# Centering two pairs of rows on the way to TensorE and applying their scale behind the matmul, in a LayerNorm, linear-attention and FFN kernel

## The chip, the cores and the metric

The kernel runs on one core of one Trainium2 chip. Five engines work side by side, each through its own queue in order: TensorE (PE, matrix products; PEld is its loading of weights), VectorE (DVE), ScalarE (ACT, functions such as Exp and Mish), GpSimd (POOL) and SyncE (SP, which here only issues DMA transfers). They wait for each other through semaphores. PE writes to PSUM, which has 8 banks of 512 float32 columns; ACT and DVE read it from there. The metric is the device time in microseconds, the median of several runs.

## The reference

One input x of 2048 rows and 448 columns (bf16) is normalized and goes through two branches that are added to it:

```python
xn = layernorm(x)                      # (x - mean) / sqrt(var + 1e-5), row by row
# A: linear attention, 16 heads of 28
q, k, v = split(xn @ wqkv)             # per head
pq, pk = q @ w_phi[h], k @ w_phi[h]
phi_q = concat(softmax(pq), softmax(-pq))
phi_k = concat(softmax(pk), softmax(-pk))
kv, z = phi_k.T @ v, sum(phi_k)
A = (phi_q @ kv) / (phi_q @ z + 1e-6) @ wo
# B: FFN with Mish
h = xn @ w1 + b1                       # 448 -> 1792
B = (h * tanh(softplus(h))) @ w2       # 1792 -> 448
out = x + A + B
```

## The kernel before

The rows lie as 16 tiles t of 128 rows; two tiles are a pair u (0 to 7). A function for each step of the work gives instructions to the engines, and the text `ORDER` (L147) names the steps one after the other: each engine's queue is the order in which the steps name it. Waits are worked out from what each instruction reads and writes (`Program.resolve`). So a step's place in `ORDER` is a place in several queues at once, and says nothing of time.

The steps, by their names in `ORDER`:

- `lx2s` and the like issue loads on SP: `lx`n rows of x from pair n on (x4 and x6 hold two pairs each), `lkm` and `lvm` rows 0 to 383 of the key and value weights, `lkt` the last 64 rows of both (loaded twice, for the upper and the lower half of the partitions, L276), `lp` the small per-head matrices, `lqT` the query weights transposed by DMA, `l1m`, `l1t`, `l2`, `lo` the FFN's and the output's weights. `lba` loads the bias.
- `z12` (`warm`, L359): twelve matmuls on a tile of zeros at the start.
- `st`u (`ln_stats`, L449): mean and variance of a pair, by bn_stats and bn_aggr on DVE; `st2b` and `st3b` do the odd tile on ACT (a Copy and a Square, each summing along the row). `rs`u (`ln_rstd`, L467): 1/sqrt(var + eps), on ACT (`a`) or POOL (`p`).
- `xn`u (`ln_pair`, L481): the normalized pair, on DVE (`d`) or POOL (`p`), in three pieces. It goes to one of four buffers xn.
- `xt`u (`xT`, L514): turns the pair into xnT, features on partitions: by PE, emptied by ACT and DVE (`b`) or by ACT (`a`), or by a DMA transpose on SP (`m`). Pairs 2 and 3 are turned by PE, six by DMA.
- `wtk`h, `wmk`h, `wmq`h (L545, L568): fold the per-head matrices into the key and query weights: Wk is turned by PE (8 transposes each for h = 0, 1), then multiplied (8 matmuls), the result emptied to Wpk or Wpq.
- `v`, `k`, `q` with a pair's number and a part (L609, L615, L677): the products of a pair with value, key and query weights; each is 28 matmuls of 64 rows by 448 columns, two of them at a time on the two halves of PE, given out in parts A (12), H (4), B (12) that may stand apart in `ORDER`. The last part's step empties the pair of banks: values by a copy (`a` on ACT, `d` on DVE), keys by two Exp on ACT (of plus and minus), written to E, and queries likewise to Eq.
- `kn`u.s (`k_norm`, L623): the key softmax's sums and reciprocals on DVE, the product on POOL. `kv`u adds the pair's part of kv; `kvz` copies it, and a DMA transpose turns it into KVZ.
- `e`t turns a tile of query exponentials by DMA; `nd`t forms numerator and denominator (16 matmuls, then DVE); `ot`u turns the result by DMA; `wo`u multiplies with wo.
- `f`q.n with parts A, H, B: the FFN's first product for half q of the rows and 128 of the 1792 features; `mish` on ACT empties it to actT. `g`t: the second product. `sto`u, `stt`t: stores.

PSUM banks are taken in pairs, the least recently used free pair first (`take2`, L380); a part holds its pair until its last step. A pair may be written again once the engines that read it have done so. Rows 6 to 13 of actT hold E until the FFN's features overwrite them, rows 4 and 5 hold Eq.

All matmuls of `v`, `k`, `q` and `f` have one line in the profile, L423 (they differ by their operands), the transposes of Wk L556, the products with the per-head matrices L580, those of xn L505.

Of the kernel before, what the change touches and what calls it, by code (L numbers as in the profile page):

```python
# [978 lines left out]
```

## Time and profile before

| what | value |
|---|---|
| median of 3 runs | 151.34 us (151.34 to 151.38) |
| span of the profiled execution, first to last instruction | 148.7 us |
| median less span | 2.6 us |
| HBM read, written | 7.02 MB, 1.84 MB |
| DVE, POOL busy in the span | 102.4 us, 38.8 us |
| the 16 DMA engines, queue q1 | 53.4% of their span |

The profile is of one execution. "Busy" counts instructions from start to end, so PE's share says that it always has a matmul in flight and not that it works at its peak. A line of a group reads: line, engine, operation, result<-operands, shapes, count, then busy time and the mean of one. In the timeline a row reads: start, time to the end of the last, engine, line, operation, count, and in brackets the idle time before it with what ended it. In the chain of waits a row reads: start, length, engine and line; from the last instruction back it follows what released each step.

### The profile page before, as it was taken

The page shows a single profiled execution, that of the slowest core. Times are in us where ns is not written, and L with a number is a line of the kernel's source. Part 1 is how long each engine was busy: PE and PEld are TensorE (multiplying, and loading weights), DVE is VectorE, ACT ScalarE, POOL GpSimd, SP SyncE. Part 2 cuts the span into 40 slices and gives each one's busy share as a digit, 9 for nine tenths or more (in the row PEclk, how much of TensorE's full clock was granted, in tenths as well). Part 3 has the DMA queues.
Part 4 walks back from the last instruction along what each step waited for, and adds up shares of the span by engine and source line. Part 5 has one row for each costly group of instructions (what it writes and reads, how often), then busy time and mean ns, then how long its engine had stood idle before and what let it go on. Part 6 is the DMA issues. An engine that isn't in the chain of part 4 may idle for free.

```text
span 148.7 us, 3867 instructions
## 1 busy us (share of the span) xinstructions
PE 144.3 (97%) x1669; PEld 74.4 (50%) x1669; DVE 102.4 (69%) x229; ACT 74.5 (50%) x91; POOL 38.8 (26%) x53
## 2 busy tenths in 40 slices
PE   6999999999999999999999999999999999999993
PEld 2375555555544554444544445545555555555562
DVE  0599898996999940407697879539983999930072
ACT  3987999879999999657757762002000000000000
POOL 4423475079999993000000000000000000000000
PEclk9999999999999999999999999999999999999999
DMA  4998678799499159399856053120013040542005
GB/s 133 240 270 232 138 143 158 128 169 334 102 194 191 30 49 132 69 223 283 225 120 121 0 66 62 27 39 0 7 21 102 20 108 0 123 100 85 4 0 185
DMA packets 39964, 17.23 MB, mean 116 GB/s; under 512 B 33932, under 2 KB 39180, under 8 KB 39948
## 3 DMA queue, kind: packets, MB, share of 16 engines
q1 hardware_dynamic: 39776, 16.89, 53.4%
q8 instruction: 13, 0.21, 0.6%
q10 hardware_dynamic: 172, 0.10, 0.2%
q14 instruction: 3, 0.02, 0.0%
HBM read 7.02 MB, written 1.84 MB: 60 GB/s over the span
## 4 chain that ended last, share of the span: by engine, by line
PE 96%; DVE 1%; POOL 0%; issue 0%; POOLq 0%
PE PS L423 50%; PE PS L828 29%; PE PS L845 7%; PE PS L364 4%; PE PS L722 3%; PE PS L649 2%; PE PS L580 1%; DVE xn L497 1%; PE PS L505 1%; DVE x_all L793 0%; POOL v_all L339 0%; PE PS L556 0%; DVE x_all L814 0%; DVE b1T L512 0%; PE PS L693 0%
## 5 line engine op out<-in xcount | busy, mean ns | idle before, releaser
L423 PE MATMUL PS<-xnT,W 64*128 64x512 bf16 x392 | 44.8, 377 | 0.0
L828 PE MATMUL PS<-W,actT 128*128 128x448 bf16 (+1 forms) x224 | 42.9, 351 | 0.0
L699 ACT ACTIVATE actT<-PS,b1T 128x1024 bf16<-128x1024 f32 x28 | 29.8, 1112 | 22.1 <-PE PS L423 22.1
L828 PEld LDWEIGHTS PS<-W,actT 128*128 128x128 bf16 x224 | 21.5, 98 | 19.8 <-issue 0.3
L423 PEld LDWEIGHTS PS<-xnT,W 64*128 64x128 bf16 x392 | 18.0, 94 | 21.9 <-PE PS L423 1.9
L630 POOL TENSOR_TENSOR actT<-actT,rSk 128x896 bf16<-128x896 bf16 x16 | 26.6, 1699 | 5.1 <-DVE rSk L628 5.1
L793 DVE TENSOR_TENSOR x_all<-PS,x_all 128x448 bf16<-128x448 f32 (+1 forms) x16 | 9.2, 614 | 15.1 <-PE PS L845 10.5
L626 DVE TENSOR_REDUCE Sk<-actT 128x32 f32<-128x896 bf16 x16 | 16.6, 1037 | 1.1 <-ACT actT L618 1.1
L618 ACT ACTIVATE actT<-PS 128x896 bf16<-128x896 f32 x16 | 13.7, 920 | 1.8 <-PE PS L423 1.7
L423 PE MATMUL PS<-Wpk,xnT 64*128 64x448 bf16 x112 | 13.2, 349 | 0.0
L423 PE MATMUL PS<-Wkv,xnT 64*128 64x448 bf16 x112 | 12.9, 349 | 0.0
L423 PE MATMUL PS<-Wpq,xnT 64*128 64x448 bf16 x112 | 12.6, 349 | 0.0
L738 DVE COPY Sq<-PS 128x16 f32<-128x16 f32 x32 | 4.0, 167 | 12.0 <-PE PS L722 12.0
L462 DVE BATCH_NORM_STATS2 stats<-x_all 128x6 f32<-128x448 bf16 x14 | 8.4, 601 | 3.5 <-DMA x_all<-in_A_x_dram 3.5
L746 DVE TENSOR_TENSOR v_all<-v_all 128x464 f32<-128x464 f32 x16 | 10.3, 642 | 0.6
L742 DVE TENSOR_TENSOR v_all<-PS,Sq 128x464 f32<-128x464 f32 x16 | 10.3, 641 | 0.5
L749 DVE TENSOR_TENSOR xn<-v_all,rden 128x448 bf16<-128x448 f32 x16 | 10.0, 626 | 0.6
L744 DVE TENSOR_TENSOR v_all<-PS,Sq 128x464 f32<-128x464 f32 x16 | 10.1, 630 | 0.0
L680 ACT ACTIVATE actT<-PS 128x896 bf16<-128x896 f32 x10 | 8.6, 930 | 0.1
L423 PEld LDWEIGHTS PS<-Wpq,xnT 64*128 64x128 bf16 x112 | 5.4, 94 | 5.0 <-ACT actT L680 0.2
L423 PEld LDWEIGHTS PS<-Wkv,xnT 64*128 64x128 bf16 x112 | 5.4, 94 | 5.0 <-ACT actT L618 0.2
L423 PEld LDWEIGHTS PS<-Wpk,xnT 64*128 64x128 bf16 x112 | 5.4, 94 | 5.1 <-issue 0.2
(83 smaller groups left out, 119.3 us busy)
## 6 DMA issues: line engine op xcount, KB each, us to landing
W<-in_B_w_dram SPq DMA_DIRECT2D x1, 1568.0 KB, 9.3
out_dram<-x_all SPq DMA_DIRECT2D x7, 224.0 KB, 2.2
W<-in_B_w_dram SPq DMA_DIRECT2D x1, 1344.0 KB, 6.5
x_all<-in_A_x_dram SPq DMA_DIRECT2D x4, 224.0 KB, 3.0
x_all<-in_A_x_dram SPq DMA_DIRECT2D x2, 448.0 KB, 4.7
Wkv<-in_A_wqkv_dram SPq DMA_DIRECT2D x2, 336.0 KB, 5.1
Wo<-in_A_wo_dram SPq DMA_DIRECT2D x2, 336.0 KB, 5.9
W<-in_B_w_dram SPq DMA_DIRECT2D x2, 224.0 KB, 3.6
```

Source lines behind the costliest of these rows:

```text
L423: ins = e.matmul(o, lhs(c, k), rhs(c, k), start=first and n == at[par][0], stop=last and n == at[par][-1])
L618: op("ACT", lambda e, s=s: e.activation(E_of(u)[:, s, :, :], two(b, D), ACT.Exp, scale=1.0 if s == 0 else -1.0), r=[pb(b), pb(b + 1)], w=[ ...
L626: op("DVE", lambda e: e.tensor_reduce(Sk[u][:, s, :], Eh(), AX.X, ALU.add), r=[("E", u, s)], w=[("Sk", u, s)], tag=f"Sk{u}.{s}")
L630: op("POOL", lambda e: e.tensor_tensor(Eh(), Eh(), ap_on(rSk[u][:, s, 0:1], [[1, 2 * H], [0, DH]]), ALU.mult), r=[("E", u, s), ("rSk", u, ...
L699: op("ACT", lambda e: e.activation(actT[:, fc, q * 1024:(q + 1) * 1024], bank(b, 2), ACT.Mish, bias=b1T[:, fc:fc + 1]), r=[("b1T",), pb(b) ...
L742: op("DVE", lambda e: e.tensor_tensor(tv(t1[i]), num(0), sx(1), ALU.mult), r=[pb(b), pb(b + 1), ("Sq", i, 1)], w=[("t1", i)], tag=f"ta{t}")
L744: op("DVE", lambda e: e.tensor_tensor(tv(t2), num(1), sx(0), ALU.mult), r=[pb(b), pb(b + 1), ("Sq", i, 0)], w=[("t2",)], tag=f"tb{t}")
L746: op("DVE", lambda e: e.tensor_tensor(t1[i], t1[i], t2, ALU.add), r=[("t1", i), ("t2",)], w=[("t1", i)], tag=f"tc{t}")
L749: op("DVE", lambda e: e.tensor_tensor(o_sb[(t // 2) % 2][:, t % 2, :].rearrange("p (h d) -> p h d", d=DH), t1[i][:, :, 0:DH], ap_on(rden[i ...
L793: op("DVE", lambda e: e.tensor_tensor(x_all[:, t, 0:n], bank(b)[:, 0:n], x_all[:, t, 0:n], ALU.add), r=[pb(b), ("x", t)], w=[("out", t)], ...
L828: ins = e.matmul(bank(b)[:, 0:width(t)], actT[:, fc, tok(t)], W2[:, fc, 0:width(t)], start=first and fc == 0, stop=last and fc == FC - 1)
L845: ins = e.matmul(bank(b)[:, 0:w], oT_of(u)[lo:hi, cc * P:(cc + 1) * P], Wo[lo:hi, cc, 0:w], start=first and n == at[par][0], stop=last and ...
```

## The change

In words:

- For pairs 2 and 3 (`CENT`) the rows are only centered (`xc`t, `center`), by DVE: x minus the mean for the even tile, x plus ACT's negative mean for the odd one. `st_mean` writes that negative mean to `nmean`. PE turns the centered pair (`ct`u, `xcT`) into row 3 of actT, emptied by ACT and DVE. Values and keys of these pairs are computed from it, and rstd is applied when they leave PSUM: values by one scaled copy for each tile, keys by four Exp with scale rstd or -rstd (`nrstd`), where there were two.
- For their queries and the FFN, pairs 2 and 3 are also normalized as before (`xn3p`, `xn2d`) and turned by DMA (`xt3m`, `xt2m`): all eight pairs now take that way.
- Statistics are given tile by tile (`sd`, `sm`, `sv` in place of `st`). The key and value weights' last 64 rows: the lower half of the partitions gets only the value part; Wk's last transposes read 64 rows, and the copy writes the result twice.
- The warm matmuls, six in place of twelve, read a constant of ones that exists from the start.
- `wmk0` and both `wmq` are emptied by ACT (before by ACT and DVE, and `wmq0` by DVE). The first empties of values are shared out anew: ACT has v3, v2, v1, v7, v5, v0 and DVE v6, v4 (before ACT v2, v3, v0, v6, v7). rstd of pairs 2, 1, 0 is on ACT, the rest on POOL; POOL normalizes pairs 3, 6, 5, DVE 1, 4, 7, 2, 0.
- A new `ORDER`. All query exponentials stand ahead of the first Mish.

The diff, cut to its core:

```diff
-pv table lx2s lba zero pm st2b lx3s lkms lps st3b lkts z12 pi b1 rs2p pw rs3a xn2d bd lx1s wtk0b lvms lx4s xn3d xt2b
-wtk1b wmk0b lqT2 xt3a v2Ha wmk1a v2Ba lqT0 st1 v3Ha lqT1 lqT3 rs1a v3Aa v2Aa st4 rs4p pk v3Ba k3H lx0s k3A qd xn1d
-wmq0d wmq1a k2H k3B lx6s pp k2A st5 q3A xn4d k2B q3B rs5p q2A xt1m l1ts q3H k1A q2H xn5p xt4m st0 v1Ad k1H st6 xt5m e7
...
+pi lx2s lba sd4 lx3s table pk z6 sm5 sv5 pw lkms xc4d b1 lps lt0s sm7 xc5d lt1s sd6 lvms pm rs2a xc7d lx1s bd lqT2
+sv7 xc6d rs3p ct2 lx6s lqT3 wtk0b lx4s wtk1b ct3 sd3 wmk0a xn3p wmk1a sd2 nr2d rs1a sd13 v3Ha xn1d sd12 v2Aa sd11 pp
+v2Ha lqT0 lqT1 v2Ba k2A rs6p k2H k3H k2B qd nr3d xn6p v3Aa k3A v3Ba wmq1a wmq0a xt1m xt3m sd10 sd8 k3B k1A lx0s v1Ha
+v1Bd xt6m sd9 k1H v1Aa sd14 q3H l1ts q3A sd15 rs4p q3B rs7p xn4d sd0 xn7d rs5p k1B xn5p sd1 xt4m q1H v6Bd v6Ad xn2d
+xt7m q1A q1B k6H k6B kn2.0 e6 v6Hd k4H kn3.1 xt2m k6A kn2.1 k4A pv k7A k4B v7Bd v7Hd rs0a kn4.0 e3 k7H q4H xn0d v7Aa
...
+k0H e9 q2B k0A q7H kn4.1 k0B v0Ad v0Ba q0H kn3.0 q0B q0A f1.3H e4 q7B q7A q5A kn1.1 q5H f1.3A e5 kn5.1 f1.2H e1 ep
+e0 kn6.1 q5B f1.3B f1.2B f0.2A f0.2H f0.0B f0.2B f0.0A f1.2A e15 kn5.0 f0.0H kn0.1 f1.13A l2s kn7.0 kn1.0 f0.1B
+f1.13H kv2 kn7.1 kv3 kv4 kn0.0 kv6 e10 kv7 kv1 kv5 kv0 f1.13B f0.12H kvz f0.1A f0.12A f0.1H f0.12B f1.8B f1.8H f1.1H
...
+sto6 sto2 sto4 stt14 g15 stt15
```

```diff
+    def load_kv_tail(eng, i):
+        (lo, hi), at = HALF[i], (0, D)[i]
+        dma(eng, lambda e: e.dma_start(Wkv[lo:hi, 3, at:2 * D], A_wqkv[384:448, D + at:3 * D]), w=[("Wt", i)],
+            tag=("ldWkv", "ldWvt")[i])
...
-                ins = e.matmul(bank(b)[:, :], ap_on(zeros[:, 0:1], [[0, P]]), ap_on(zeros[:, 0:1], [[0, TCW]]), start=True,
-                               stop=True)
+                ins = e.matmul(bank(b)[:, :], ap_on(ones, [[0, P]]), ap_on(ones, [[0, TCW]]), start=True, stop=True)
...
+    def st_mean(t):
+        i = t // 2 % 2
+        op("ACT", lambda e: e.activation(junk[i][:], x_all[:, t, :], ACT.Copy, scale=-1.0 / D, accum_out=nmean[:, t:t + 1]),
+           r=[("x", t), ("junk", i)], w=[("nm", t), ("junk", i)], tag=f"sm{t}")
...
+    def center(t, eng):
+        u = t // 2
+        for n, (lo, hi, at) in enumerate(parts_of_row(t)):
...
+            op(eng, lambda e, lo=lo, hi=hi, at=at: e.tensor_scalar(
+                xn[u % NXN][:, at:at + hi - lo], x_all[:, t, lo:hi], mean_of(t), None, op0=mean_op(t)),
+               r=[("x", t), mean_res(t)], w=[("xn", u % NXN, t % 2, n)], tag=f"xc{t}.{n}")
...
+    def xcT(u):
+        i = u % NXN
+        b = take2(False)
+        pe(lambda e: transpose7(e, b, xn[i], 3), [("xn", i, 0, 0), ("xn", i, 1, 0), ("xn", i, 1, 1), ("ident",)],
+           [pb(b), pb(b + 1)], f"xT{u}c")
+        for eng, lo, hi, bb, n in (("ACT", 0, 3, b, 0), ("DVE", 3, 7, b + 1, 1)):
+            at = (u % 2) * 7 * P
+            evac(eng, lambda lo=lo, hi=hi: actT[:, CROW, at + lo * P:at + hi * P],
...
+                    n = 64 if 2 * h + c == 3 else P
+                    ins = e.transpose(oT(c, n)[:, g, :], Wk[0:n, 2 * h + c, g * GP:(g + 1) * GP], ident[0:n, 0:n])
...
+    def scaled(eng, dst, src, t, r, w, tag):
+        if eng == "ACT":
+            op("ACT", lambda e: e.activation(dst(), src(), ACT.Copy, scale=rstd[:, t:t + 1]), r=r, w=w, tag=tag)
...
     def k_mm(u, part):
         def then(b):
+            if u in CENT:
+                for s in range(2):
+                    for i in range(2):
+                        op("ACT", lambda e, s=s, i=i: e.activation(
+                            E_of(u)[:, s, i, :], bank(b + i)[:, 0:D], ACT.Exp,
+                            scale=(rstd, nrstd)[s][:, 2 * u + i:2 * u + i + 1]),
+                           r=[pb(b + i), ("rstd", u), ("nrstd", u)], w=[("E", u, s)] if i else [("Eh", u, s)],
+                           tag=f"exkc{u}.{s}{i}")
+                return
```

More of the change, by code (lines that the diff above doesn't have):

```diff
@@ L227, in _kernel, with xcT_of @@
     FE = FC - NU
+    CENT = (2, 3)
+    CROW = 3
+    def xcT_of(u, c):
+        return actT[:, CROW, (u % 2) * 7 * P + c * P:(u % 2) * 7 * P + (c + 1) * P]
     def E_of(u):
@@ L607, in tok_works, with cent_works, works_of, turned @@
                            lambda c, k: W[k[0]:k[1], c, :]) for par in range(2)]
+    def cent_works(u, W):
+        return lambda b: [(bank(b + par)[:, 0:D],
+                           lambda c, k, par=par: xcT_of(u, xchunk(c, par))[k[0]:k[1]],
+                           lambda c, k: W[k[0]:k[1], c, :]) for par in range(2)]
+    def works_of(u, W):
+        return cent_works(u, W) if u in CENT else tok_works(u, W)
+    def turned(u):
+        return [("xcT", u, 0), ("xcT", u, 1)] if u in CENT else [("xnT", u), ("xnU", u)]
+    def scaled(eng, dst, src, t, r, w, tag):
+        if eng == "ACT":
+            op("ACT", lambda e: e.activation(dst(), src(), ACT.Copy, scale=rstd[:, t:t + 1]), r=r, w=w, tag=tag)
+        else:
+            op("DVE", lambda e: e.tensor_scalar(dst(), src(), rstd[:, t:t + 1], None, op0=ALU.mult), r=r, w=w, tag=tag)
     def v_mm(u, part, eng):
         def then(b):
+            if u in CENT:
+                for i in range(2):
+                    scaled(eng, lambda i=i: v_all[:, u, i, :, 0:DH],
+                           lambda i=i: bank(b + i)[:, 0:D].rearrange("p (h d) -> p h d", d=DH), 2 * u + i,
+                           [pb(b + i), ("rstd", u)], [("v", u, i)], f"vec{u}.{i}")
+                return
             evac(eng, lambda: v_all[:, u, :, :, 0:DH], lambda: two(b, D).rearrange("p i (h d) -> p i h d", d=DH),
-                 [pb(b), pb(b + 1)], [("v", u)], f"ve{u}")
-        pair_part(f"v{u}", part, tok_works(u, Wv), [("xnT", u), ("xnU", u)] + rows_of("Wv"), then)
+                 [pb(b), pb(b + 1)], [("v", u, 0), ("v", u, 1)], f"ve{u}")
+        pair_part(f"v{u}", part, works_of(u, Wv), turned(u) + (rows_of("Wv") if part in "FH" else [("Wv", 0)]), then)
     def k_mm(u, part):
         def then(b):
+            if u in CENT:
+                for s in range(2):
+                    for i in range(2):
+                        op("ACT", lambda e, s=s, i=i: e.activation(
[3 more added lines that the diff above has]
+                           tag=f"exkc{u}.{s}{i}")
+                return
             for s in range(2):
@@ L620, in then @@
                    r=[pb(b), pb(b + 1)], w=[("E", u, s)], tag=f"exk{u}.{s}")
-        pair_part(f"k{u}", part, tok_works(u, Wp[1]), [("xnT", u), ("xnU", u)] + [("Wp", 1, h, c) for h in range(2) for c in range(2)], then)
+        pair_part(f"k{u}", part, works_of(u, Wp[1]), turned(u) + [("Wp", 1, h, c) for h in range(2) for c in range(2)], then)
     def k_norm(u, s):
@@ L867, in _kernel @@
     for u in range(NU):
-        add(f"st{u}", ln_stats, u)
-        add(f"st{u}b", ln_stats, u, True)
+        for t in (2 * u, 2 * u + 1):
+            add(f"sd{t}", st_dve, t)
+            add(f"sm{t}", st_mean, t)
+            add(f"sv{t}", st_var, t)
+            add(f"xc{t}d", center, t, "DVE")
+            add(f"xc{t}p", center, t, "POOL")
+            if by_act(t):
+                add(f"xc{t}a", center, t, "ACT")
+        for eng, c in (("DVE", "d"), ("POOL", "p")):
+            add(f"nr{u}{c}", neg_rstd, u, eng)
+        add(f"ct{u}", xcT, u)
         add(f"xt{u}b", xT, u, "both")
@@ L911, in _kernel @@
             add(f"l{n}m{c}", load_main, eng, "W" + n, t, A_wqkv[:, (i + 1) * D:(i + 2) * D])
-        add(f"lkt{c}", load_tail, eng, "Wkv", Wkv, A_wqkv[:, D:3 * D])
+        for i in range(2):
+            add(f"lt{i}{c}", load_kv_tail, eng, i)
         add(f"l1m{c}", load_main, eng, "W1", W1, B_w1)
```

135 lines of the change are left out of this document (72 added, 63 removed).

## The prediction

> **What bounds the kernel now.** I read the page, the chain of waits, then the timeline engine by engine over the first 60 us, and last the windows of ACT.
>
> ```profile
> span 148.7 us, 3867 instructions
> ...
> PE 144.3 (97%) x1669; PEld 74.4 (50%) x1669; DVE 102.4 (69%) x229; ACT 74.5 (50%) x91; POOL 38.8 (26%) x53
> ...
> ACT  3987999879999999657757762002000000000000
> ```
>
> TensorE (PE) is busy 97% of the span. ACT's 50% is an average: over the first 16 slices (60 us) it is at nine tenths, afterwards nearly idle. The chain of waits, in order of time:
>
> ```profile
> 1.39 5.30 PE PS L364 x12
> ...
> 7.02 1.06 DVE xn L497 x3
> ...
> 8.69 0.45 PE PS L556 x8
> 9.14 0.40 PE PS L580 x8
> 9.53 0.39 PE PS L505 x7
> ...
> 10.72 3.32 PE PS L423 x34
> 14.04 0.89 PE PS L580 x16
> 14.94 36.24 PE PS L423 x370
> 51.18 0.88 PE PS L649 x96
> ...
> 145.69 0.56 DVE x_all L793
> ```
>
> From 14.94 to 145.69 PE alternates only between kinds of matmul, so the time is PE's work plus what PE loses before about 15 us. The last 3.0 us (145.69 to 148.7: one addition and a store) stay: both orders end with g15 and stt15. I call **lost** all time up to an instant that isn't useful PE work at full speed. One matmul of 448 columns on half the rows costs 0.094 us, since six move the next start by 0.57:
>
> ```profile
> 19.42 0.73 PE L423 MATMUL PS<-Wkv,xnT 64*128 64x448 bf16 x6
> 19.99 0.35 PE L423 MATMUL PS<-Wpk,xnT 64*128 64x448 bf16 x2
> ```
>
> Up to 14.94 the useful work is 16 transposes of Wk (0.9), two pairs turned (0.78), 32 matmuls at L580 (1.7) and 36 at L423 (3.4): 6.8 us, so 8.1 are lost. At 51.18, where the first kv group starts, 42.7 of work are done: 24 units of v, k and q less one of 14 matmuls (322 x 0.094 = 30.3), six FFN units (14 matmuls of 512 columns, 0.1075 by their width: 9.0), the rest 3.4. Lost: 8.5. So PE loses only 0.4 more in 36 us, rounding included.
>
> **The change, part by part.** *The way to the first turned pair.*
>
> ```profile
> 3.54 0.63 DVE L462 BATCH_NORM_STATS2 stats<-x_all 128x6 f32<-128x448 bf16 x1 [3.54 <-DMA x_all<-in_A_x_dram]
> 6.94 1.13 DVE L497 TENSOR_SCALAR xn<-x_all,mv,rstd 128x448 bf16<-128x448 bf16 x3
> 6.99 0.82 PE L556 MATMUL PS<-ident,Wkv 128*112 128x128 bf16 x8 [0.18 <-DMA Wkv<-in_A_wqkv_dram]
> 7.84 0.60 ACT L510 ACTIVATE Eq<-PS 112x512 bf16<-112x512 bf16 x1 [0.46 <-PE PS L556]
> 8.53 0.61 PE L556 MATMUL PS<-ident,Wkv 128*112 128x128 bf16 x8
> ```
>
> Before, pair 2 waits for statistics of both rows, rstd and three normalizing parts (end 8.07). Now xc4d follows its own statistics at 4.3 and xc5d needs only ACT's mean: three parts 1.13 and b1's copy 0.1, so ct2 can start at 5.6. The waits that this adds are met: ACT's mean 5 is there at 4.2, b1, in front of xc5d on DVE, leaves PE at about 3.7, and rstd 2 is done at about 6.4, long before the first scaled copy. The Wk transposes still wait for Wk's landing (6.99; the loads ahead of it are the same three). So ct2 goes into idle PE time, and behind wtk0 follow wtk1 (four of its eight transposes are half as wide, 0.1 saved, the only PE work that changes) and ct3, without the hole before 8.13.
>
> *Fewer warm matmuls.* Six instead of twelve, from about 0.85, end at 3.5. Row L364 gives 5.30/12 = 0.44 us for 512 columns; the 8 transposes at 6.99 took 0.82 to their end and those at 8.53 only 0.61 (start to start 0.107 and 0.056 us in the slow and the fast part). So PE ran at half speed until about 7.4, six us after its first matmul and with almost no gap. Now PE works 2.6 us, stands idle to 5.6, turns pair 2 (0.75 slow), stands again to 6.99. At half speed wtk0, wtk1, ct3, wmk0 and wmk1 take 3.75 instead of 1.9 us, to 10.75, and then v3's tail and v2 (16 matmuls, 1.5) follow without a gap. Full speed returns at 9.7 at the earliest (6.0 less the 3.3 of work that went before, counted from 6.99), at 13.0 at the latest (6.0 from 6.99). By the same steps as below that is 151.5 and 153.0. I take 10.8, nearer the early end because half of that work has been done, later than it because of the idle time between.
>
> By the Trainium skill, "TensorE: Matmul & The Clock Gate", Part 1 (the HAM clock gate), PE gets its full clock only after a free-running window of about 3.4 us that was busy, wherever the window falls. By that rule six matmuls cannot fill one, and the stretch from 6.99 does so between 10.4 and 13.8: 151.7 to 153.4 as an estimate. The trace agrees with six us of slow work, and holds one phase only.
>
> *Start of the dense work.* ACT's rows:
>
> ```profile
> 4.47 0.67 ACT L458 ACTIVATE junk<-x_all,rmean 128x448 bf16<-128x448 bf16 x1
> 5.14 0.56 ACT L453 ACTIVATE junk<-x_all 128x448 bf16<-128x448 bf16 x1
> 6.85 0.29 ACT L476 ACTIVATE lnv<-mv,eps_col 128x2 f32<-128x2 f32 x1
> 7.18 0.20 ACT L478 ACTIVATE rstd<-lnv 128x2 f32<-128x2 f32 x1
> 8.73 0.49 ACT L510 ACTIVATE xnT<-PS 128x384 bf16<-128x384 bf16 x1 [0.29 <-PE PS L505]
> 10.89 0.93 ACT L510 ACTIVATE Wpk<-PS 128x896 bf16<-128x896 f32 x1
> 14.97 0.98 ACT L510 ACTIVATE Wpq<-PS 128x448 bf16<-128x448 f32 x2 [0.49 <-PE PS L580]
> 22.56 3.35 ACT L618 ACTIVATE actT<-PS 128x896 bf16<-128x896 f32 x4
> 41.87 1.28 ACT L699 ACT_TABLE_LOAD   x1
> 43.37 4.13 ACT L699 ACTIVATE actT<-PS,b1T 128x1024 bf16<-128x1024 f32 x4 [0.21 <-PE PS L423]
> ```
>
> ACT's statistics end at 7.4 as before (same operations). Then come ct2's copy, two of Wk^T, ct3's, wmk0 and wmk1 (ACT alone empties them now), rs1a: 0.45, 0.5, 0.5, 0.45, 0.8, 0.9, 0.55 from start to start. With PE at full speed from 7.4 the keys' weights are ready at 11.0, PE starts k2 at 11.1 with 3.9 us of work done, and ACT starts on v2 at 11.55: **lost 7.2**. With full speed at 10.8 each copy waits for slower transposes; v2's matmuls end at 12.3, k2 follows, ACT starts on v2 at 12.5: **lost 8.4**.
>
> *ACT from there to the kv group.* PE can't open a fifth pair of banks before ACT or DVE has emptied the first, so it cannot run away from ACT. The new order needs all exponentials, the one table load and three Mish before kv2 gets its banks (kv2 takes those of f1.2). ACT's pitch is 0.44 for 448 columns (0.98 less 0.54), 0.81 for 896, 1.0 for a Mish. Sixteen of 448 (v2, v3, k2, k3, both wmq: 7.0), 32 of 896 (v1, v7, v5, v0, six k, eight q: 25.9), rs0a 0.5, table 1.3, three Mish 3.1: 37.8 us, and some 0.7 in which ACT waits for PE (0.45 ahead of k2, the rest at k7 and q4). New beside before: rstd as a scale by partition in twelve of them. Its price isn't in the trace. The nearest rows are those with a bias by partition: 0.67 against 0.56 us (L458, L453) and 0.29 against 0.20 (L476, L478), so 0.09 each, 1.1 in all; the other end is nothing. I take the middle.
> From 12.5 ACT is through at 51.0 to 52.1. Before kv2 PE has 42.4 of work: all 24 units (31.6), four FFN units and three parts (7.5), the rest 3.3. It would be there at 12.3 + 38.5 = 50.8. So PE waits 0.2 to 1.3, mostly for the banks of wmq, v1, k7 and kv2.
>
> *The rest.* Eight pairs now go through the DMA transpose instead of six. On SP x6 moves ahead of x4 and lands at about 11, where the load in its place did:
>
> ```profile
> 14.39 1.63 SPq L517 DMA_TRANSPOSE xnT<-xn  x1
> ...
> xnT<-xn SPq DMA_TRANSPOSE x6, 3.1
> ```
>
> On DVE xn1d stands behind row 13's statistics, which wait for x6, and behind rs1a, done at 12.4; so xt1m goes out at about 13.3 and lands at 16.4, ahead of k1 (17), SP's queue being free then. xt3m and xt6m follow by 1.3 and 4 us and are wanted 2 and 4 after k1. If one is late, PE waits at that place for as long; there is no other work in front of it. The two table loads that go (all Mish now follow all exponentials) pay for part of ACT's additions, and the sum above holds that. POOL normalizes 16 half pairs of keys:
>
> ```profile
> 29.55 1.70 POOL L630 TENSOR_TENSOR actT<-actT,rSk 128x896 bf16<-128x896 bf16 x1 [4.37 <-DVE rSk L628]
> 32.01 24.88 POOL L630 TENSOR_TENSOR actT<-actT,rSk 128x896 bf16<-128x896 bf16 x15 [0.76 <-DVE rSk L628]
> 59.59 1.83 DVE L660 TENSOR_SCALAR KVT<-PS,epsT 30x224 bf16<-30x224 f32 x4 [6.01 <-PE PS L649]
> 61.46 1.23 SPq L666 DMA_TRANSPOSE KVZ<-KVT  x1
> ...
> KVZ<-KVT SPq DMA_TRANSPOSE x1, 3.2
> ```
>
> They took 26.6 and ended 2 us before their last kv. Now DVE reaches kn2.0 some 13 us after ct3's copy (statistics, four normalizations), about 23, so POOL could end at 51 without a gap, 54 with waits for k4 and k6; kv0 wants it at 54. I take no loss and keep 0.8 for the range. KVZ needs 0.2 + 1.8 + 3.2 us after kv0, and the new order has 5.5 of FFN work there: covered by 0.3 us where it was covered by 8.
>
> **Sum.** Lost 8.4 plus 0.2 to 1.3 is 8.6 to 9.7, against 8.5: +0.1 to +1.2, middle +0.65, less 0.1 of work: +0.55. The span becomes 149.3; with the 2.6 us between 148.7 and the median of 151.34, that makes 151.9.
>
> **Rivals.** *The clock is full in time (faster).* Place: the transposes of Wk at 6.99. If they run at 0.056 us each, lost is 7.2 and ACT starts at 11.55; ACT, waiting 0.5 for PE, is then through at 49.9 to 51.0, PE at 11.1 + 38.5 = 49.6: lost 7.5 to 8.6, with 0.1 less work -1.1 to 0, middle -0.55: 150.8. It decides where the clock comes back before about 9: from there on ACT, not PE, sets 11.55. For it: one phase is all that the trace shows, and pair 2's turn and wtk0 are new early work. Against: twelve matmuls with no gap barely sufficed. A scale by partition for nothing brings a late clock half way to it. *Cold, but ACT pays nothing for the scale (no change).* Lost 8.4 + 0.2, less 0.1: 151.3. *POOL or KVZ is late, or the clock later still (much slower).* Lost 8.4 becomes 9.5 at 13.0, or kv0 waits 0.8: 152.7 to 153.0. That the change doesn't do what it says, centred rows with the scale behind the matmul, I rule out from the diff: only u = 2, 3 change.
>
> **How the numbers follow.** Forecast with the much slower cases 0.44, faster rival 0.38, no change 0.18; under 0.2% (0.3 us) this kernel's measurement tells nothing from no change. The faster case spans 150.2 to 151.3, and the range takes all of it but its lower end: 150.4. Above it ends at 152.9, the clock back at 12 (+0.6) with the upper half of the scale's price (+0.4); beyond lies POOL's wait on top. The forecast's own range is 151.5 to 152.9.
>
> **What would show it.** Right: 8 transposes at L556 from 6.99 at 0.107 us, matmuls of the first v at half speed, k2 starting after 12, ACT gapless to q5, PE's loadings waiting for ACT in the row of waits. Wrong: transposes at 0.056 us, k2 before 11.3, exponentials of 448 columns at 0.54 us, or PE idle before kv0 by POOL. Wrong altogether: a hole in PE after 60 us.

## The result, and the profile after

The changed kernel takes 169.67 us (168.31 to 170.38) against 151.36 us: a ratio of 1.120 (95% interval 1.114 to 1.125). The forecast was 151.9 with a range to 152.9. The direction was right, the size some thirty times too small. The span grew by 17.8 us, from 148.7 to 166.5. Times here are medians of all runs, while a ratio leaves out runs more than 1.5% above the fastest of the same kernel: two of four with pair 0 early and W1 right behind it (171.87 and 172.78 us remain), one each in four other kernels, and three of four with W2 late, which so has no ratio.

The page of the changed kernel (first lines, busy tenths of PE, granted clock, chain by engine):

```profile
span 166.5 us, 3875 instructions
...
PE 151.8 (91%) x1663; PEld 73.3 (44%) x1663; DVE 103.7 (62%) x231; ACT 75.7 (45%) x100; POOL 41.6 (25%) x56
...
PE   6699899987998944999999999999999999999993
...
PEclk9999999999999995699999999999999999999999
...
PE 72%; DMA 8%; DVE 8%; issue 4%; SPq 4%; ACT 3%; ACTq 0%
```

PE is busy for 7.5 us more than before with 6 instructions fewer, and it has holes: digits 4 and 4 in the 15th and 16th slice (58 to 67 us), with the clock reduced in the 16th and 17th. (The clock's row reads 9 up to its first recorded change, here at 11.78 us; how fast PE ran before that shows in the starts of its matmuls.) The chain, which before alternated between kinds of matmul from 15 us on, now leaves PE again and again:

```profile
13.85 4.79 DMA xnT<-xn
...
32.75 3.15 DVE xn L512 x3
...
37.28 0.96 DVE v_all L558
...
49.05 3.42 DMA EqT<-actT
...
58.81 1.26 PE PS L737 x124
60.07 3.08 issue
63.16 1.69 PE PS L737 x118
64.84 1.77 issue
66.61 0.24 PE PS L737 x4
```

The windows show the same by stage (length, then busy us and count for PE, PEld, DVE, ACT, POOL; granted clock; DMA share; GB/s). First the kernel before, then the changed one:

```profile
12.00:51.00 39.00, 39.00 (x408) 19.63 (x404) 35.84 (x73) 35.88 (x43) 28.34 (x30) 1.00 0.79 169
51.00:59.00 8.00, 8.00 (x281) 4.30 (x279) 2.52 (x5) 7.96 (x10) 5.97 (x5) 1.00 0.52 74
59.00:68.00 9.00, 9.00 (x152) 4.32 (x136) 2.14 (x7) 5.90 (x6) 0.00 (x0) 1.00 0.90 173
```

```profile
12.00:51.00 39.00, 36.02 (x354) 15.62 (x352) 34.07 (x69) 33.40 (x50) 27.06 (x30) 1.00 0.93 171
51.00:59.00 8.00, 7.26 (x101) 3.02 (x95) 4.88 (x8) 7.20 (x8) 8.00 (x6) 1.00 1.00 216
59.00:68.00 9.00, 4.15 (x254) 3.00 (x237) 1.07 (x3) 0.71 (x1) 0.83 (x2) 0.72 0.62 123
```

Between 12 and 51 us PE gets through 54 matmuls fewer although it looks 92% busy: a PE that waits for its own last matmul is counted as busy. That wait is visible only in the row of PE's weight loads. First before, then after (what waited, for what; us in all, times, longest):

```profile
PEld PS L423 <- PE PS L423: 1.9, 6, 0.3
```

```profile
PEld PS L435 <- PE PS L435: 13.9, 29, 0.6
```

Its source is in the code: a unit (one pair's product, or one `f`q.n) is given out in parts A, H and B; part B works on the same two banks as A and H, from the other half of PE, and `pe_pass` (L415 of before, `after=`) lets it start only when PE's own last matmul of that unit has ended. The old order never puts B beside A or H of the same unit; the new one does so 28 times, which is called a place below. From start to start such a step takes 0.41 us instead of 0.19 (448 columns), about 0.225 us more. (Read in the rows: a part A or B is 6 matmuls, H is 2, a unit 14; the description of the kernel above gives twice that.)

**Where the 17.8 us lie.** The first group of keys and values starts at 58.8 us with 42.4 us of work done: 16.4 lost by the forecast's count of work, against 8.5 before (+7.9; the forecast had +0.1 to +1.2). In the row of groups 4.85 us are lost (3.08 and 1.77 above), behind it some 1.5 us at half clock (66.85 to 69.80), and the remaining 3.5 us would fit the 14 places behind it, a reading that the experiments below do not bear out alone.

### The profile page after: what moved, and what is told of

It is laid out like the page before. It is cut to its first block, busy times and chain, and to the rows that moved or that the text cites. A ratio compares the mean times of both kernels' runs of the same rounds, so it can differ in the third digit from the quotient of the medians.

```text
span 166.5 us, 3875 instructions
## 1 busy us (share of the span) xinstructions
PE 151.8 (91%) x1663; PEld 73.3 (44%) x1663; DVE 103.7 (62%) x231; ACT 75.7 (45%) x100; POOL 41.6 (25%) x56
## 4 chain that ended last, share of the span: by engine, by line
PE 72%; DMA 8%; DVE 8%; issue 4%; SPq 4%; ACT 3%; ACTq 0%
PE PS L435 33%; PE PS L916 25%; PE PS L933 7%; SPq L776 3%; DMA xnT<-xn 3%; DMA Wkv<-in_A_wqkv_dram 3%; DVE xn L512 3%; DVE Sk L714 2%; PE PS L810 2%; DMA EqT<-actT 2%; PE PS L737 2%; DVE v_all L558 1%; PE PS L612 1%; ACT actT L768 1%; ACT actT L706 1%
## 5 line engine op out<-in xcount | busy, mean ns | idle before, releaser
L435 PE MATMUL PS<-xnT,W 64*128 64x512 bf16 x392 | 48.5, 386 | 1.4 <-ACT actT L768 0.7
L718 POOL TENSOR_TENSOR actT<-actT,rSk 128x896 bf16<-128x896 bf16 x16 | 26.8, 1700 | 8.6 <-DVE rSk L716 8.3
L435 PEld LDWEIGHTS PS<-xnT,W 64*128 64x128 bf16 x392 | 17.5, 96 | 26.0 <-PE PS L435 5.7
L881 DVE TENSOR_TENSOR x_all<-PS,x_all 128x448 bf16<-128x448 f32 (+1 forms) x16 | 9.6, 617 | 26.8 <-PE PS L916 26.8
L435 PE MATMUL PS<-Wpq,xnT 64*128 64x448 bf16 x112 | 13.8, 350 | 0.3
L435 PE MATMUL PS<-Wkv,xnT 64*128 64x448 bf16 x84 | 11.0, 351 | 1.9 <-DVE v_all L558 1.5
L706 ACT ACTIVATE actT<-PS 128x896 bf16<-128x896 f32 x12 | 10.4, 924 | 0.9 <-PE PS L435 0.9
L435 PE MATMUL PS<-Wpk,xnT 64*128 64x448 bf16 x84 | 10.3, 350 | 0.5 <-DMA xnT<-xn 0.4
L768 ACT ACTIVATE actT<-PS 128x896 bf16<-128x896 f32 x10 | 8.6, 920 | 1.3 <-DMA EqT<-actT 0.8
L748 DVE TENSOR_SCALAR KVT<-PS,epsT 30x224 bf16<-30x224 f32 x4 | 1.8, 448 | 10.9 <-PE PS L737 10.9
```

The costliest lines, as they stand in the source:

```text
L435: ins = e.matmul(o, lhs(c, k), rhs(c, k), start=first and n == at[par][0], stop=last and n == at[par][-1])
L706: op("ACT", lambda e, s=s: e.activation(E_of(u)[:, s, :, :], two(b, D), ACT.Exp, scale=1.0 if s == 0 else -1.0), r=[pb(b), pb(b + 1)], w=[ ...
L718: op("POOL", lambda e: e.tensor_tensor(Eh(), Eh(), ap_on(rSk[u][:, s, 0:1], [[1, 2 * H], [0, DH]]), ALU.mult), r=[("E", u, s), ("rSk", u, ...
L768: op("ACT", lambda e, s=s: e.activation(Eq_of(u)[:, :, s, :].rearrange("p i (h n) -> p i h n", n=64)[:, :, :, 0:QP], two(b, D).rearrange(" ...
```

## The experiments

Suspects: (1) parts side by side; (2) eight groups in one row, where PE runs out of instructions, with W2's load beside it; (3) the clock behind such a hole; (4) pair 0's normalizing on DVE, late and slow, and what is late after it; (5) six warm matmuls; and against all of them the centering itself. Edits are in `ORDER` alone. Each kernel stands against the kernel before on the same chip (151.1 to 151.5).

### The order or the centering

The changed kernel's operations in the order of the kernel before, with q3 and q2 behind the first products of pair 1, where their transposes have landed; twelve or six warm matmuls. Four steps also go back to the engine that the kernel before gives them: pair 6's normalizing and pair 5's values to DVE, pair 6's values to ACT, pair 0's rstd to POOL:

```diff
-... z6 ... v3Ha xn1d sd12 v2Aa sd11 pp v2Ha lqT0 lqT1 v2Ba k2A ... kv2 kn7.1 kv3 kv4 kn0.0 kv6 e10 kv7 kv1 kv5 kv0 ...
+... z12 ... k3B rs5p k1A xt4m v1Ha l1ts xn2d k1H sd0 v1Ba xn5p k1B sd1 xt2m sd12 v1Aa xt5m q3H q3A ... q1A sd15 rs7p rs6p
+(then as before from k4A on, q2 in the place of q1)
```

> The changed kernel's operations (two pairs centred only, scale behind the matmul), twelve warm matmuls, and the order of the kernel before from k4 on, with q2 and q3 put where their DMA transposes have landed. Theory that the order costs the time and the centring does not: no B part stands beside an A or H part of its unit, the groups of the keys and values come in lots of 3, 3 and 2 with W2's load behind them, so the span is 148 to 151.5 and the time 150.5 to 154. Rival, the centring itself (twelve scaled copies and exponentials, two more DMA transposes, DVE's extra work) costs: PE then waits on ACT, DVE or DMA before 55 us by several us, time over 156.

> The same as the kernel with twelve warm matmuls and the old order, with six of them. Theory of the clock: full speed comes 3 to 4.5 us later (about 11.8 instead of 7.4) and PE's lost time grows by 1.2 us: slower than the twelve by 0.8 to 1.5 us. Rival: ACT's chain sets the start of the dense work, the clock is hidden: within 0.4 us.

Measured: 152.85 us with twelve (1.011, 1.006 to 1.016), 154.24 with six (1.018, 1.011 to 1.025). The kernel with six differs from the changed kernel by the order and those four steps, so of the 18.3 us they make 15.4; the six warm matmuls make 1.4, with intervals that overlap, and 1.5 stay with the centering in this order. The windows of the kernel with twelve show PE full again where the changed kernel had its holes:

```profile
12.00:51.00 39.00, 37.02 (x368) 20.04 (x366) 32.19 (x68) 35.32 (x48) 25.27 (x29) 0.96 0.90 176
51.00:59.00 8.00, 8.00 (x256) 4.43 (x254) 5.50 (x9) 7.97 (x9) 8.00 (x6) 1.00 0.49 43
59.00:68.00 9.00, 9.00 (x144) 4.12 (x142) 1.79 (x4) 5.97 (x7) 1.01 (x2) 1.00 0.81 118
```

From the last group on its trace takes 86.9 us to the last matmul, as in the kernel before to 0.01 us; all that it loses lies ahead of the groups (54.2 instead of 51.1 us). In that trace the clock fell back for 3.4 us; in the other three runs the mean granted clock is 1.00.

The trace with six warm matmuls reaches the first group at 54.9 us and is 14.0 us shorter than the changed kernel's. Of these 14.0 us, 3.9 lie ahead of the groups (58.8 against 54.9) and 5.3 are the holes in the row of groups (by the starts around them); the other 4.8, an estimate by the count of matmuls, lie almost all behind it. So about half of the 7.7 us by which the changed kernel's first group is late (58.8 against 51.1) comes with the old order too.

### Parts side by side

The clean price: the kernel before, with 20 such places made behind 70 us and nothing else (the first two):

```diff
-f1.8B f0.9H f1.8A f1.8H nd0 f0.11B f0.9A f0.11A f0.11H
+f1.8B f1.8A f0.9H f1.8H nd0 f0.11B f0.11A f0.9A f0.11H
```

> The kernel before with 20 places behind 75 us where a B part follows an A or H part of the same unit directly (none before); nothing else is changed. Theory: each costs PE about 0.225 us, since the next part's weights wait for PE's own last matmul, and PE has nothing to make it up with: 20 x 0.225 = 4.5 us, time 155 to 156.5. Rival: the engines behind PE were setting the pace there or PE catches up: less than 1 us.

Measured: 156.12 us (1.033, 1.030 to 1.036): 4.8 us, 0.24 each, as the theory had it. Its waits:

```profile
PEld PS L423 <- PE PS L423: 9.4, 18, 0.6
```

Now the reverse, all 28 places of the changed kernel taken apart by moving one part a place or a few, and only the 14 behind the groups:

> The changed kernel with 25 steps of its order moved by a few places, so that no part B of a unit stands directly beside a part A or H of the same unit on TensorE (28 such places before, none in the old order); nothing else changes. Theory: at each such place TensorE waits for its own last matmul of the part before, about 0.225 us (start to start 0.41 in place of 0.19): 28 x 0.225 = 6.3 us less, 163.4 us, and no gap of 0.41 us left in the trace. Rival: TensorE is held by ScalarE there anyway, the gaps come back as waits for banks: 168 us or more.

> The changed kernel with the 14 places behind the keys' and values' last group where a B part stands beside an A or H part taken apart by moving one part a place or two; everything up to there is as it was. Theory: there PE is the bound, each place costs 0.24 us as in the kernel before with 20 such places: 14 x 0.24 = 3.4 us, 166.3 plus or minus 0.7. Rival: DVE or ACT sets the pace there, as it did when all 28 places were taken apart: less than 1 us.

Measured: 171.99 us (1.135, 1.131 to 1.138) and 170.26 us (1.126, 1.122 to 1.131): nothing won; both theories missed, and the rivals' times came. The traces tell why. The waits for PE itself shrink (from 13.9 us to 3.7 with all places apart, to 8.8 with the 14), but PE now runs into DVE, which needs 3 us for each numerator (nd), here with the 14 apart:

```profile
85.10 1.25 PE L435 MATMUL PS<-xnT,W 64*128 64x512 bf16 x10 [1.60 <-DVE v_all L832]
```

Ahead of the groups it is ACT and the query transposes: in the changed kernel and in the one with all 28 apart, the chain passes ACT at 41.7, SP's issues, a transpose at 49.1 and ACT again at 52.5 us, and the first group starts at 58.8 us in both. Two things blur the comparison: the holes in the row of groups are 6.1 and 6.3 us in these two traces (with the 14 and with all apart) instead of 4.85, and with all 28 apart the clock stays at half for 10.2 us instead of 6.8. So the places cost 0.24 us where PE is the bound, and in the changed kernel other waits lay right under them.

### The row of groups, W2 and the clock

The kernel before with its eight groups, given out there as 3, 3 and 2, in one row (W2 stays behind); the changed kernel with W2's load moved behind `kvz`; and with the groups spread as 3, 3 and 2:

```diff
-kv5 kn7.1 e0 kv0 kv2 q7A q5A f0.13A q5H f0.13B kv7 kv4 e10 kv6 ... f0.10B kv3 kv1
+kv5 kv0 kv2 kv7 kv4 kv6 kv3 kv1                                  (before, one row)
-f1.13A l2s kn7.0 ... kvz f0.1A        +f1.13A kn7.0 ... kvz l2s f0.1A     (after, W2 late)
-kv2 kn7.1 kv3 kv4 kn0.0 kv6           +kv2 kn7.1 kv3 kv4 kn0.0 f0.1A f0.1H f1.1H f1.1B f0.12H f1.1A kv6  (after, spread)
```

> The kernel before with its eight kv groups put in one row (they stood 3, 3 and 2), W2's load behind them as it was. If the row alone empties the instructions: one or two gaps of 1 to 2 us each inside the row, 152.4 to 155. If it takes W2's load on its way: no gap, 151.2 to 151.8.

> The changed kernel with the issue of W2's load (1.5 MB) moved behind kvz, so that it isn't on its way while the eight kv groups run in a row. If the row of groups alone empties TensorE's instructions, a gap or two of 1 us or more stay, and 1 to 4 us are won at most. If W2's load makes the fetch late, both gaps go, and 5 to 7 us are won: 163 to 165.

> The changed kernel with its eight kv groups in three lots (3, 3, 2) with 2.6 to 2.8 us of other matmuls between them, as the old order has them, in place of eight in a row; nd3, nd2 and nd0 stand a few parts later. The load of W2 stays ahead of them. Theory (instructions): eight groups are 512 instructions in 2.4 us, and TensorE runs out of instructions (the gaps of 3.3 and 2.0 us that wait for nothing the profile shows). Spread, both gaps go, and with them the clock's fall at 63.0: 5.2 + about 1.5, so 162.5 to 164.5. Rival (the load of W2 holds the fetch up, however the groups stand): gaps of 2 to 3 us stay while W2 is on its way, 167 or more.

Measured: 155.52 us (1.028, 1.023 to 1.033) for the row in the kernel before, a little over the 152.4 to 155 expected; 166.79 (163.94 to 168.47) with W2 late, too wide a spread for a verdict; 169.02 (1.114, 1.110 to 1.119) spread, where 162.5 to 164.5 was expected. PE's rows of the groups, first in the kernel before as it was (no holes), then in the first two runs, with holes ended by "issue", that is by nothing that the profile shows:

```profile
51.11 0.95 PE L649 MATMUL PS<-actT,v_all 128*30 128x56 bf16 x96
54.77 0.95 PE L649 MATMUL PS<-actT,v_all 128*30 128x56 bf16 x96
58.77 0.68 PE L649 MATMUL PS<-actT,v_all 128*30 128x56 bf16 x64
```

```profile
55.91 2.18 PE L649 MATMUL PS<-actT,v_all 128*30 128x56 bf16 x205 [0.80 <-ACT actT L680]
60.59 0.57 PE L649 MATMUL PS<-actT,v_all 128*30 128x56 bf16 x51 [2.50 <-issue]
```

```profile
58.42 1.18 PE L737 MATMUL PS<-actT,v_all 128*30 128x56 bf16 x124
60.92 1.22 PE L737 MATMUL PS<-actT,v_all 128*30 128x56 bf16 x128 [1.32 <-issue]
64.65 0.21 PE L737 MATMUL PS<-actT,v_all 128*30 128x56 bf16 x4 [2.51 <-issue]
```

A group is 32 matmuls, some 9 ns from start to start, with 32 loadings; eight in a row are 512 instructions in 2.4 us. In the changed kernel's window from 59 to 67 us the queue of instructions moves just two packets of 16 KB:

```profile
q8 instruction: 2, 0.03, 1.7%
```

By the Trainium skill, "Runtime: NRT & Kernel Launch", section on instruction fetch mechanics, an engine's instructions come in blocks of 16 KiB (256 instructions) over a DMA queue of its own, at a cost that is mostly hidden. The trace agrees in the blocks; in these rows the cost isn't hidden: 2.5 us in one hole without W2's load, 3.8 in two with W2 late (1.32 and 2.51), 4.85 in two with W2 on its way.

That the holes are waits for instructions shows in two more things. Between the two holes of a kernel lie 128 matmuls with 128 loadings, which is one block of 256. And each hole ends at the same distance behind a packet on that queue: packets move at 60.7 and 64.3 us in the changed kernel, 58.6 and 62.0 with W2 late, 58.1 with the row in the kernel before, and in all eight traces that have such holes (14 of them) PE goes on 2.3 to 2.6 us after one. With W2 late the first packet moves 0.15 us after the row begins, in the changed kernel 1.9 us after: that is W2's part. POOL's products, the other thing that the groups need, had all ended 1.4 us or more before the end of every hole (59.7 against 63.2 us in the changed kernel).

Spread, one hole of 1.1 us stays, but the gain is given back: the FFN parts put between the groups were missing later between the numerators, which I had also left too close, and PE waited for DVE at 74 to 82 us, with the clock at half for 3.4 us behind it. The 4.1 us of the row in the kernel before are not the hole alone: a wait of 0.80 us for ACT stands ahead of the row, one place came with the edit, and in two of its four runs the granted clock was 0.989.

In the changed kernel the granted clock is half from 62.98 to 69.80 us, from the end of the first hole on; in the run with W2 late from 65.98 to 69.39. No run changes the clock alone, so its part, some 1.5 us, is worked out from the trace and not measured.

### Pair 0, DVE beside POOL, and W1

In the changed kernel DVE normalizes pair 0 while POOL multiplies keys. The three parts, and POOL's row beside them; then the same three parts for pair 1 in two kernels of the old order, once beside POOL's normalizing and memsets, once with POOL idle (the first kernel under "What the centering costs by itself"):

```profile
32.66 3.24 DVE L512 TENSOR_SCALAR xn<-x_all,mv,rstd 128x448 bf16<-128x448 bf16 x3
```

```profile
30.16 3.35 POOL L718 TENSOR_TENSOR actT<-actT,rSk 128x896 bf16<-128x896 bf16 x2 [3.52 <-DVE rSk L716]
```

```profile
11.72 2.15 DVE L512 TENSOR_SCALAR xn<-x_all,mv,rstd 128x448 bf16<-128x448 bf16 x3
```

```profile
11.71 0.89 DVE L512 TENSOR_SCALAR xn<-x_all,mv,rstd 128x448 bf16<-128x448 bf16 x3 [0.62 <-ACT rstd L490]
```

By the Trainium skill, "Advanced Engine Details and Errata", mode summary of VectorE's performance modes, POOL's instructions and DVE's two-port ones block each other. The rows agree: 0.89 us alone, 2.15 and 3.24 beside POOL.

Pair 0's steps were moved ahead: first with W1 right behind, then with pairs 0 and 5 ahead of W1:

```diff
-rs0a kn4.0 e3 k7H q4H xn0d ... xt5m q6H e7 q4A q6A xt0m k5H l1ms
+sd0 sd1 ... q1H rs0a ... kn2.0 xn0d ... xt2m xt0m l1ms ... xt5m q6H e7          (first)
+sd0 sd1 ... q1H rs0a ... kn2.0 xn0d ... xt2m xt0m xt5m ... e2 ... e7 l1ms       (then)
```

> The changed kernel with row pair 0 normalised right behind the first two sums of the keys (DVE, about 25 us instead of 32.7) and its DMA transpose and W1's load moved ahead with it. Theory: the three parts took 3.24 us in the changed kernel because POOL multiplied keys at that time, and v4's copy, the transpose of pair 0, W1 and then the query transposes came late; so the parts take 0.9 to 2 us, the hole of PE at 36.4 us (1.65) and the one at 53.2 us (0.9) go, and the span falls by 1.5 to 3 us: 166.7 to 168.2. Rival: the first 58 us are set by ACT and the waits between parts anyway: the holes move, the time stays at 169 to 170.

> The changed kernel with row pair 0 normalised early, as in the run that came out slower, but with the DMA transposes of pairs 0 and 5 ahead of W1's load, and W1 behind the query transpose e7. Theory: W1's load holds back every transpose queued behind it by 4 to 6 us; in the earlier run that was pair 5 (landed 40.9, PE waited 5.3 us). With it ahead of W1 that hole goes: 166.7 to 168.5. Rival: pair 0 early doesn't pay at all, or another wait takes its place: 169 to 171, and over 172 if W1 isn't the cause.

Measured: 173.86 us (1.140, 1.134 to 1.146), then 168.27 (1.106, 1.100 to 1.113). The first was expected at 166.7 to 168.2 and came out slower than the changed kernel; the second is in its range. In the first, PE stood still for 4.9 us: SP's rows show W1's load, two query transposes whose issue takes 6.4 us behind it, and only then pair 5's:

```profile
30.59 0.59 SPq L281 DMA_DIRECT2D W<-in_B_w_dram  x1
31.23 6.39 SPq L776 DMA_TRANSPOSE EqT<-actT  x2
37.67 1.30 SPq L563 DMA_TRANSPOSE xnT<-xn  x1
```

```profile
41.06 0.56 PE L435 MATMUL PS<-Wpk,xnT 64*128 64x448 bf16 x2 [4.94 <-DMA xnT<-xn]
```

With pair 5 ahead of W1 that hole is gone and the first group starts at 56.7 instead of 58.8 us: 2.0 won. Only 1.4 are left in the time by the medians, as the holes in the row of groups grew from 5.3 to 7.3 us (by the starts of the matmuls around them).

### All suspects at once

The changed kernel in its own order with twelve warm matmuls, pair 0 and W1 as in the last run, the groups as 3, 3 and 2 with W2 behind, and the numerators spaced:

```diff
-z6 ... l2s kn7.0 ... kv2 kn7.1 kv3 kv4 kn0.0 kv6 e10 kv7 kv1 kv5 kv0 f1.13B f0.12H kvz
+z12 ... kv2 kn7.1 kv3 kv4 kn0.0 f0.1A f0.1H f1.1H f1.1B f0.12H f1.1A kv6 e10 kv7 kv1
+f1.13B f0.12A f1.8B f0.12B f1.8H kv5 kv0 kvz l2s
```

> The changed kernel in its own order with four things mended: twelve warm matmuls, pair 0 normalised and turned early with W1 behind it, the groups of the keys and values in three lots with FFN parts between and W2's load behind them, and the numerators and denominators (nd) spaced by 2.75 us of PE work so that DVE keeps up. The 27 places where a B part stands beside an A or H part stay. Theory: 2 us of the early chain, 5 us of holes in the row of groups, 1.5 to 2 us of half clock and 1 us of warm-up go: 158 to 161. Rival: the holes come back elsewhere, as in the earlier runs with one thing mended: over 164.

> The same with those 27 places taken apart too. Theory: now nothing else covers them, and each is worth up to 0.24 us as in the kernel before: 27 x 0.24 = 6.5 us at most, 4 to 6.5 expected: 152.5 to 156. Rival: other engines set the pace by then and they stay worth nothing, as in the two runs with the rest unmended: within 1.5 us of the kernel with the places left.

Measured: 178.44 us (1.178, 1.173 to 1.183) and 179.38 (1.186, 1.182 to 1.190). 158 to 161 and 152.5 to 156 were expected. The front was as expected (last group at 64.7 instead of 66.6 us, no hole in the row), but I had put W2 ahead of two query transposes and the numerators too late for the output parts. The chain of the first:

```profile
68.74 4.60 SPq L776
73.38 5.70 DMA EqT<-actT
...
132.97 2.90 DMA Wpk<-xn
...
144.29 2.92 DMA WqT<-xn
```

Both were mended:

```diff
-kvz l2s f1.8A e11 f1.6H f1.6B e14 ... wo5H g7 nd15 ot7m g6 g10 nd13 ot6m g11 sto3 wo6A nd9 wo7H wo2H wo2B wo2A
+kvz f1.8A e11 f1.6H f1.6B e14 l2s ... wo5H g7 nd15 ot7m g6 sto3 wo2H wo2A nd13 ot6m wo2B g10 nd9 g11 sto5 g4 nd8
```

> The changed kernel with the same mends as in mended, and its two new waits mended too: W2's load behind the last early query transposes e11 and e14 instead of ahead of them (their landing cost a hole of 2.8 us), and the output parts (wo) and second FFN products (g) in an order that fits the later nd (waits of 4.0 and 6.4 us at the end, with the clock halved behind them). 24 parts stand side by side. Theory: 158 to 161, as first expected of mended. Rival: over 164, a further wait that single runs haven't shown.

> The same with the 24 places taken apart. Theory: 24 x 0.24 = 5.8 us at most, 3 to 5.8 expected. Rival: DVE (nd) and ACT (exponentials) cover them: under 1.5 us.

Measured: 160.89 us (1.062, 1.058 to 1.068), as expected, and 162.70 (1.075, 1.071 to 1.079), not as expected. So suspects 2 to 5 together are 8.8 us of the 18.3, in which four places fewer and the new order of numerators and output parts are included. With the 24 places taken apart the part behind the last group shrinks from 92.2 to 90.4 us (9 places fewer, 0.2 each), as the price says; ahead of the groups a query transpose comes late, and with it ACT's exponential behind it: PE waits 2.4 us at 37 us, its clock falls back, and the first group starts at 60.1 instead of 56.8. What separates 160.9 from the 152.9 of the old order with twelve warm matmuls is divided only in part. In the traces 2.9 us lie up to the last group (65.2 against 62.3) and 5.3 behind it (92.2 against 86.9); of these 5.3 the nine places are 1.8 and a wait for a transpose at 139.6 us is 0.9. What the rest is stays open.

### What the centering costs by itself

In the trace of the kernel with the old order and twelve warm matmuls PE waited 1.4 us for pair 1's transpose, and its clock fell back for 3.4 us. Three attempts to mend its head: POOL's normalizing behind pair 1's (with the copy of the query weights, `qd`, right behind it); then `qd` behind row 8's statistics; then pair 3's scaled copies and pair 1's values on DVE (`v3Bd`, `v1Ad`), run once more for its trace, since the first traced execution took 304 us, twice the timed ones:

```diff
-rs1a sd8 v3Ha xn1d v2Aa ... sd9 pp pv v3Aa v2Ba k2A k2H qd nr3d v3Ba        (old order, twelve)
+rs1a ... v3Ha xn1d v2Aa qd v2Ha xn3p nr3d xt1m v3Aa v2Ba sd8                (first)
+rs1a ... v3Ha xn1d v2Aa xt1m v2Ha xn3p nr3d lx0s v3Aa v2Ba sd8 k2A k2H qd   (second)
+... qd v3Bd sd9 ... v1Ad sd12 xt5m rs0p l1ts q3H q3A xn0d sd13 xt0m         (third)
```

> The kernel with centred rows, twelve warm matmuls and the old order, with its two holes at the head mended: POOL normalises pair 3 only after DVE has normalised pair 1 (in that kernel the three parts on DVE took 2.15 us beside POOL instead of 0.9, and the DMA transpose of pair 1 landed 1.6 us late, after which PE's clock fell back for 3.4 us), row pair 6 is loaded behind that transpose, and the doubled query weights come before the statistics of row 9. Theory: the holes of 0.66 and 1.57 us and the 1.3 us at half clock go, 2.5 to 3.5 us: 149.3 to 150.5, faster than the kernel before by 0.5 to 1.3%. Rival: the transpose lands late for the DMA rings' sake and not DVE's: no more than 1 us is won, 151.8 to 153.

> The centred rows in the old order again, with the transpose of pair 1 early (as in the last run of that kind, where it landed in time and the clock stayed full) and the copy that doubles the query weights behind the statistics of row 8 instead of ahead of them, so that POOL and DVE get pairs 3 and 4 ready in time, and rows 0 and 6 loaded behind the first transposes. Theory: the holes of that run at 14.0, 19.2, 22.5 and 24.6 us (4.6 in all) came from DVE standing 2.2 us for the query weights; they go, 149.0 to 150.5. Rival: the transposes land late whatever DVE does, since eight of them and four loads share the rings by then: over 151.

> The last kernel with centred rows in the old order, but with the scaled copies of pair 3 and the copy of pair 1's values on DVE instead of ACT (2.2 us off ACT, which had no gap from 12.5 to 31 us), and pair 0 normalised and turned 1.5 to 2 us earlier. Theory: the remaining holes of PE (0.63, 0.29, 0.53 behind ACT, 0.79 behind pair 0's transpose) go: 150.0 to 151.2, no slower than the kernel before. Rival: DVE is as full as ACT there, and the holes move to the transposes that wait for it: 152 to 153.5.

> The last kernel with centred rows in the old order once more, for its trace, which the other run of it didn't give (its profiled execution took twice the timed ones). Time as timed, 155 to 156. If DVE is as full as ACT at the head (the rival that won), PE's holes lie before 35 us and are released by DVE or by transposes that waited for DVE. If they lie elsewhere, the rival falls too.

Measured: 153.38 us (1.015, 1.011 to 1.018), 152.75 (1.010, 1.007 to 1.013), 155.45 (1.026, 1.024 to 1.029) and 155.21 in the run for the trace. None of the three came to the 149 to 151.2 us that the theories had. In the first the old hole went and the clock stayed full, but DVE now stood for the query weights:

```profile
14.83 0.23 DVE L299 COPY WqT<-WqT 128x256 bf16<-128x256 bf16 x1 [2.23 <-DMA WqT<-in_A_wqkv_dram]
```

and the transposes behind it came late (PE holes of 0.5 to 1.6 us at 19 to 26 us). In the second ACT has no gap over 0.2 us from 12.5 to 31 us, PE still waits 0.4 to 0.6 us in three places, and the first group starts at 53.3 instead of 51.1 us. In the third the chain runs mostly on DVE from 12 to 34 us (in the second to 25), as the rival had it, but PE's longest holes end with ACT (1.1 us at 26.8, another 1.1 at 46.5); a transpose and DVE end only 0.4 and 0.3 us (30.6 and 31.8), and the time rises. So DVE's being full is not shown as the whole cause. No version of mine with centred rows beats the kernel before; whether one could is open.

## Why the prediction was wrong

- **The step that failed** is "Before kv2 PE has 42.4 of work ... It would be there at 12.3 + 38.5 = 50.8. So PE waits 0.2 to 1.3". It counted matmuls at the pitch of the old order and checked only ACT against them. The first group came at 58.8, 8.0 us later. Of the new order I followed ACT's queue, but not DVE's, SP's transposes, nor what `pe_pass` makes B wait for, which stands in the code and in the row "PEld ... <- PE" of before (1.9 us, 6 times). What the runs showed in its place: with the same operations and six warm matmuls in the old order the first group comes at 54.9, 3.8 later than before; the new order adds 3.9, of which pair 0 and W1 moved ahead give 2.0 back. Taking the places apart gave nothing there (58.8), so they are not shown as the cause ahead of the groups.
- **The sum's last line** took everything behind as dense, as before. "Wrong altogether: a hole in PE after 60 us" was the test, and that is what came: 4.85 us of holes from a row of groups that before was broken into three lots. The listing of the new `ORDER` shows the row, and the old trace has no hole there, so its price could not be read from it, only suspected. The hole needs no more than the row itself: 2.50 us in the kernel before.
- **"xt1m goes out at about 13.3 and lands at 16.4, ahead of k1 (17)"**: it went out at 13.85 and landed at 18.6, and PE waited 0.42 us by its row. DVE's three parts took 1.45 us beside POOL instead of 0.9, and the transpose itself 4.8 instead of 3.1.
- **POOL**: "I take no loss" for its products held (no wait of PE on them), but the step asked only when POOL ends, not what its products do to DVE beside them, 3.24 instead of 0.89 us.
- **W1 and the query transposes** were not in the working at all. W1 was issued at 37.2 instead of 31.5 us, and the query transposes behind it came so late that ACT waited 0.77 us for one and began its pass only at 52.5.
- **The clock**: the transposes of Wk at half speed, k2 after 12 us (13.02) and full speed at 11.78 lie in the bounds (9.7 to 13.0), one us past the value taken. Six warm matmuls cost 1.4 us in the pair of kernels that differ by nothing else, with intervals that overlap; the forecast's 8.4 less 7.2 made it 1.2. That the clock falls back behind a later hole was left out.
- **The scale by partition**: the upper end was right. 448 columns without and with it (Wpq's passes start 0.42 us apart, the scaled ones of keys and values 0.52 to 0.53):

```profile
17.96 1.88 ACT L556 ACTIVATE Wpq<-PS 128x448 bf16<-128x448 f32 x4
...
19.66 1.23 ACT L699 ACTIVATE actT<-PS,rstd 128x448 bf16<-128x448 f32 x2
```

- **The rivals** all priced the head and POOL; none had a mechanism of the order itself, where 15 of 18 us lay. A rewritten order of 359 steps should have had a rival of its own.

## What to carry to other kernels

When a change brings a new order, the old profile's pitch is no price for it: go through the new list for each engine and look for neighbours that the old list never has (two parts of one unit, eight small groups in a row, a large load ahead of small transposes), then price each one by a kernel that has only that. Taking one suspect out of a slow kernel says little while others wait right under it; putting one suspect into the fast kernel gave each clean price here (0.24 us for a place; 2.5 us for the hole in the row of groups, 4.1 with what moved beside it).

## What the runs showed of the hardware

- PE can run out of instructions: 256 matmuls of 56 columns with their weight loads in one row cost 2.5 us of holes in the kernel before and 3.8 to 7.0 in the changed one, the more with a load of 1.5 MB on its way; the same groups in lots of three, with 2.8 us of other work between, cost nothing in the kernel before.
- After such a hole the clock is halved for one to three stretches of 3.4 us (65.98 to 69.39 with W2 late, 62.98 to 69.80 in the changed kernel, 62.80 to 73.04 with all places apart). The hole of 2.50 us in the kernel before left the clock full in the traced run, while in the old order with twelve warm matmuls holes of 0.50 and 1.40 us, ending at 14.91 and 17.95, were enough (half from 17.83 to 21.25): the length of one hole doesn't decide it. By the Trainium skill, "TensorE: Matmul & The Clock Gate", Part 1 (the HAM clock gate), the window is 3.4 us and free-running. The lengths agree. From that rule I had concluded that six warm matmuls cannot fill a window; in five traces full clock came at 11.4 to 11.8 us, but in two (groups spread, pair 0 with W1 behind pair 5) it came at 4.15 and 3.6 us for one window and then fell back until 11.0 and 10.4. There the measurement decides against my conclusion. With twelve it came at 4.0 to 7.4 us.
- DVE's normalizing took 0.89 us alone and 1.45 to 3.24 us beside POOL.
- The issue of DMA transposes behind a load of 1.3 MB (W1) took SP 6.4 us for two, against 2.6 for two at 13.85 us in the changed kernel.
